# Attention and highway layer on one core: queries in 1 KB rows, transposes by row half, score and state matmuls mixed anew, a new order of work

## The chip, the cores and the metric

The kernel runs on one core of a Trainium2 chip. The core has a matrix engine (PE; its weight loads are shown apart as PEld), a vector engine (DVE), a scalar engine (ACT), a third elementwise engine (POOL) and a queue engine (SP) that issues transfers; 16 DMA engines move the data. The metric is the device time of one execution in microseconds. Before the change it was 109.42 us (median of 3 runs, 109.22 to 109.61).

## The reference, cut to what matters

Inputs: `q`, `k`, `v` of shape (4, 8, 768, 64), a decay `lam` per head, and two 512 x 512 weight matrices with a bias. Everything is float32.

```python
for b in range(nb):                       # blocks of 64 positions
    intra = (qb @ kb.T) * Dmask           # Dmask[i, j] = lam ** (i - j) for i >= j
    intra = intra @ vb
    inter = (qb * lam ** (pos + 1)) @ kv_state
    out[:, :, block] = intra + inter
    kv_state = lam ** 64 * kv_state + (kb * lam ** (63 - pos)).T @ vb
x = out as (3072, 512)                    # 4 batches x 768 positions, 8 heads x 64
H = relu(x @ w_h);  T = sigmoid(x @ w_t + b_t)
result = T * H + (1 - T) * x              # = x + T * (H - x)
```

The block length of 64 doesn't bind: the kernel scales q by `lam**t` and v by `lam**-t` and uses blocks of 128 positions.

## The kernel before, in words

**Tiles.** One tile is 256 positions of one batch with all 8 heads; there are 12 (n = 0 to 11, three in a row belong to one batch). Head pairs (`hp`, 4 of them) share the 128 partitions, `e` is the head within a pair. Position `2p + j` lies on partition p, so the upper and lower 64 partitions are the two blocks of 128 positions (`b`).

**Steps of a tile**, by their tokens: `Lk`, `Lq`, `Lv` load a half (four heads, 256 KB) each, in rows of 512 bytes. `CK` casts k to bf16, `CQ` and `CV` scale and cast q and v; most stand on POOL. `TK`, `TQ` (line 209) turn k and q on PE with eight 128 x 128 transposes each, and `EK`, `EQ` copy them out of PSUM. `SS.n.e` (lines 222 and 227) issues 16 score matmuls of one `e` in turn with 16 state matmuls of one block; each of these uses a quarter of the array. `KE` copies the running state out (512 columns, half of them zeros, so that one full-array matmul serves a head pair). `M` (line 261) masks the scores on DVE, four per tile. `I` (line 277) is q times the state, `A` (line 287) masked scores times v, both added in PSUM; `D` copies the sum into `xT`. `F` (line 305) is the highway layer: eight matmuls of 256 columns for half the output features `u` and one weight matrix `w`; `G` is the sigmoid on ACT, `H` and `X` the rest on DVE. `R` (line 352) turns the result back by matmuls with an identity on half the rows of the array each, `E` copies it out and `ST` stores 512 KB. The last tile is handled in two halves of 128 positions (F.11 and F.12).

**Order.** A string, `PLAN`, lists all tokens; each engine issues its own in that order and waits on the others by semaphores. A number behind `=` is the PSUM bank. All loads and stores go through SP's queue. `Z` (line 371) are matmuls on zeros that do no work of the kernel. The buffers of each kind are counted in `BUFS`.

Of the kernel before, what the change touches and what calls it, by code (L numbers as in the profile page):

```python
# [22 lines left out]
WC.0.1.0@POOL D.0.1@ACT Lv.2.1 WC.0.1.1@DVE Z.4=0 SS.1.0=01 M.1.1.1 I.1=35 KE.1.1@ACT Lv.2.0 F.0.0.0=4 WC.1.1.0@DVE PT
M.1.0.1 Lk.3.1 F.0.1.0=6 M.1.0.0 WC.1.0.0@POOL WC.1.0.1@ACT Lk.3.0 WC.1.1.1@DVE A.1.1 A.1.0 BC F.0.0.1=1 H.0.1 Lq.3.1
D.1.1@ACT H.0.0 D.1.0@ACT F.0.1.1=0 Lq.3.0 CQ.2.2@POOL F.1.0.0=2 Lv.3.0 G.0.1@ACT CK.2.2@DVE F.1.0.1=6 Lv.3.1
G.0.0@ACT X.0.1@DVE TQ.2.2=5 Lq.4.0 X.0.0@DVE TK.2.2=4 EQ.2.2@ACT CV.2.2@POOL F.1.1.0=3 Lq.4.1 EK.2.2@DVE G.1.0@ACT
H.1.0 SS.2.0=01 Lk.4.1 H.1.1 CK.3.2@POOL SS.2.1=54 Lk.4.0 M.2.0.1 F.1.1.1=2 KE.2.0@ACT M.2.1.0 Lv.4.0 TK.3.2=3 M.2.1.1
CQ.3.2@POOL G.1.1@ACT I.2=15 M.2.0.0 Lv.4.1 A.2.1 X.1.0@DVE A.2.0 Lk.5.0 R.0=40 D.2.0@ACT D.2.1@DVE CV.3.2@POOL
TQ.3.2=6 E.0.0@ACT Lk.5.1 F.2.1.1=1 E.0.1@ACT EQ.3.2@DVE Lq.5.1 EK.3.2@ACT X.1.1@DVE F.2.1.0=5 CQ.4.2@POOL Lq.5.0
R.1=40 H.2.1 SS.3.1=62 Lv.5.0 F.2.0.0=3 CK.4.2@POOL KE.3.0@ACT M.3.1.1 Lv.5.1 E.1.1@ACT M.3.1.0 SS.3.0=52 E.1.0@ACT  # L30
H.2.0 Lq.6.0 TQ.4.2=0 KE.3.1@ACT CV.4.2@POOL M.3.0.1 TK.4.2=6 G.2.1@ACT Lq.6.1 F.2.0.1=4 M.3.0.0 EQ.4.2@ACT EK.4.2@DVE
Lv.6.0 I.3=32 A.3.0 CK.5.2@POOL A.3.1 Lk.6.1 SS.4.1=56 D.3.0@ACT D.3.1@DVE TK.5.2=0 KE.4.0@ACT M.4.1.1 Lk.6.0
F.3.0.0=2 G.2.0@ACT CQ.5.2@POOL EK.5.2@DVE Lv.6.1 SS.4.0=36 H.3.0 F.3.0.1=0 Lq.8.0 M.4.0.0 CV.5.2@POOL M.4.0.1
TQ.5.2=2 Lk.9.0 G.3.0@ACT F.3.1.0=3 X.2.1@DVE Lq.7.0 EQ.5.2@ACT X.2.0@DVE F.3.1.1=6 CQ.6.2@POOL M.4.1.0 Lq.7.1
KE.4.1@ACT I.4=14 H.3.1 G.3.1@ACT R.2=25 Lk.8.1 X.3.0@DVE A.4.0 E.2.1@ACT X.3.1@DVE A.4.1 Lk.7.1 SS.5.0=30 E.2.0@ACT
D.4.0@DVE CK.6.2@POOL SS.5.1=56 D.4.1@ACT Lk.7.0 TQ.6.2=2 M.5.0.0 KE.5.0@ACT CV.6.2@POOL TK.6.2=1 M.5.1.1 Lv.7.0
EQ.6.2@ACT F.4.1.0=4 M.5.0.1 Lv.7.1 EK.6.2@ACT F.4.0.0=3 H.4.1 Lk.8.0 M.5.1.0 I.5=62 SS.6.1=01 H.4.0 Lq.8.1 A.5.0
KE.6.0@ACT M.6.1.0 CQ.7.2@POOL R.3=45 Lv.9.1 A.5.1 M.6.1.1 SS.6.0=30 D.5.0@ACT Lv.8.0 F.4.0.1=1 M.6.0.0 D.5.1@ACT
M.6.0.1 Lk.9.1 TQ.7.2=6 G.4.0@ACT CK.7.2@POOL F.5.0.0=3 Lq.10.1 EQ.7.2@ACT F.4.1.1=2 H.5.0 Lk.10.1 E.3.1@ACT X.4.0@DVE
# [26 lines left out]
def kernel(  # L66
# [31 lines left out]
    def copy(eng, dst, src):  # L98
        if eng == "ACT":
            A.activation(dst, src, AF.Copy)  # L100
        else:
            ENG[eng].tensor_copy(dst, src)  # L102


    lam_bc = singles.tile([128, H], F32)
    A.dma_start(out=lam_bc, in_=lam.partition_broadcast(128))
# [4 lines left out]
    blank = singles.tile([128, 512], BF16)  # L111
    V.memset(blank, 0.0)
# [53 lines left out]
    def get(*key):  # L166
        return made[key]
# [256 lines left out]
```

## Time and profile before

| | |
|---|---|
| median of 3 runs | 109.42 us |
| profiled execution, its span | 107.8 us |
| PE busy, of the span | 100.5 us, 93% |
| DVE, ACT, POOL busy | 83.4, 70.1, 55.6 us |
| moved by DMA | 27.6 MB, 256 GB/s over the span |

The profile is one execution. The span runs from the first to the last instruction of the program; the runs' times hold 1.6 us more than it (109.42 - 107.8). The chain of waits follows the work back from the last instruction. Each of its rows has a start, a length and the work. In the groups of instructions a row ends with the busy time, the mean length of one, and the idle time before them with what ended it. A matmul's own length there (some 200 to 270 ns) is latency, since matmuls are pipelined; what one costs in a stream is read from the lengths of the pieces in the chain.

### The profile page before, as it was taken

The numbers are of one execution on the slowest core, as the hardware profiler recorded it, in microseconds if no ns is written. First come the engines' busy times: TensorE is split into PE (matmuls) and PEld (weight loads), VectorE is DVE, ScalarE is ACT, GpSimd is POOL, SyncE is SP. The second block draws the span as 40 slices with busy tenths as digits, with TensorE's granted clock in tenths as the row PEclk, the third lists the DMA queues.
The fourth block names the chain that finished last, engine by engine and source line by source line (L and its number), as shares of the span: only waits on it lengthen the run. The fifth ranks groups of instructions, "written<-read, shape, count | busy, mean of one in ns | idle before, by whom it ended". The sixth has DMA issues, their size and how long they took to land.

```text
span 107.8 us, 4970 instructions
## 1 busy us (share of the span) xinstructions
PE 100.5 (93%) x2190; PEld 81.0 (75%) x2190; DVE 83.4 (77%) x140; ACT 70.1 (65%) x129; POOL 55.6 (52%) x46
## 2 busy tenths in 40 slices
PE   4998999999999999999999999999999899999950
PEld 1333655488987888889889889889898688899940
DVE  1053495879699987999995997999977978958860
ACT  2213347485875588499669758957697778587940
POOL 6028342127889887985468593999770600000000
PEclk9999999999999999999999999999999999999996
DMA  1799999999999999999999999999979334108264
GB/s 29 191 304 289 292 356 389 324 292 266 288 288 263 312 295 291 276 291 281 292 298 285 272 360 309 306 289 342 355 220 317 141 138 158 43 6 316 79 239 150
DMA packets 42701, 27.59 MB, mean 256 GB/s; under 512 B 1588, under 2 KB 38712, under 8 KB 42680
## 3 DMA queue, kind: packets, MB, share of 16 engines
q1 hardware_dynamic: 42528, 27.27, 86.7%
q8 instruction: 17, 0.28, 1.1%
q14 instruction: 4, 0.03, 0.1%
q10 hardware_dynamic: 152, 0.01, 0.1%
HBM read 20.98 MB, written 6.29 MB: 253 GB/s over the span
## 4 chain that ended last, share of the span: by engine, by line
PE 74%; DVE 10%; DMA 5%; issue 3%; POOL 1%; SPq 1%; ACT 1%; POOLq 0%; DVEq 0%
PE bt L305 18%; PE bh L305 17%; PE bs L222 7%; PE bx L352 6%; PE bo L287 6%; DMA qf<-in_q_dram 5%; DVE m L261 5%; PE bqtr L209 5%; PE bspin L371 5%; PE bktr L209 4%; PE bo L277 3%; DVE hm L310 2%; DVE th L323 2%; PE kv L227 2%; POOL qb L195 1%
## 5 line engine op out<-in xcount | busy, mean ns | idle before, releaser
L305 PEld LDWEIGHTS <-w_b 128*128 128x128 bf16 x416 | 36.4, 98 | 5.3 <-issue 0.9
L261 DVE TENSOR_TENSOR m<-bs,tri 128x512 bf16<-128x512 f32 x48 | 31.1, 683 | 2.8 <-PE bs L222 2.6
L195 POOL TENSOR_TENSOR qb<-qf,pow_q 128x1024 bf16<-128x1024 f32 (+1 forms) x13 | 23.5, 1810 | 9.4 <-DMA qf<-in_q_dram 8.7
L319 ACT ACTIVATE bt<-bt,bt_col 128x256 f32<-128x256 f32 (+1 forms) x52 | 22.0, 432 | 7.9 <-PE bt L305 4.4
L305 PE MATMUL bt<-xT,w_b 128*128 128x256 bf16 (+1 forms) x208 | 24.5, 265 | 0.7 <-issue 0.5
L305 PE MATMUL bh<-xT,w_b 128*128 128x256 bf16 (+1 forms) x208 | 25.0, 265 | 0.0
L195 POOL TENSOR_TENSOR vs<-vf,pow_v 128x1024 bf16<-128x1024 f32 x10 | 19.0, 1903 | 8.8 <-DMA vf<-in_v_dram 6.4
L310 DVE SCALAR_TENSOR_TENSOR hm<-bh,xT 128x512 bf16<-128x512 f32 (+1 forms) x26 | 16.5, 644 | 3.3 <-PE bh L305 2.4
L323 DVE TENSOR_TENSOR th<-bt,hm 128x512 bf16<-128x512 f32 (+1 forms) x26 | 16.5, 644 | 2.1 <-ACT bt L319 2.0
L371 PE MATMUL bspin<-blank,id 128*128 128x512 bf16 x45 | 13.4, 447 | 1.4 <-POOL id masks.py:199 1.4
L222 PE MATMUL bs<-qT,kT 64*64 64x128 bf16 x384 | 13.9, 218 | 0.4 <-PE bspin L371 0.2
L100 ACT ACTIVATE ss<-kv 128x512 bf16<-128x512 f32 x15 | 9.0, 597 | 7.5 <-PE bs L222 6.3
L102 POOL CAST kb<-kf 128x1024 bf16<-128x1024 f32 (+1 forms) x10 | 9.9, 994 | 6.0 <-DMA kf<-in_k_dram 6.0
L222 PEld LDWEIGHTS <-kT 64*64 64x64 bf16 x384 | 10.9, 106 | 2.6 <-issue 1.1
L100 ACT ACTIVATE xT<-bo 128x512 bf16<-128x512 f32 x16 | 9.2, 597 | 4.4 <-PE bo L287 4.4
L100 ACT ACTIVATE o<-bx 128x512 f32<-128x512 f32 x19 | 10.5, 596 | 1.3 <-PE bx L352 1.3
L100 ACT ACTIVATE qT<-bqtr 128x1024 bf16<-128x1024 bf16 (+1 forms) x10 | 9.8, 980 | 1.8 <-PE bqtr L209 1.8
L371 PEld LDWEIGHTS <-id 128*128 128x128 bf16 x45 | 4.5, 110 | 7.1 <-issue 2.8
L287 PE MATMUL bo<-m,vs 64*64 64x128 bf16 x384 | 9.1, 219 | 0.4 <-DVE m L261 0.4
L227 PE MATMUL kv<-vs,kb 64*64 64x64 bf16 x320 | 9.3, 196 | 0.0
L100 ACT ACTIVATE kT<-bktr 128x1024 bf16<-128x1024 bf16 (+1 forms) x7 | 6.8, 970 | 2.1 <-PE bktr L209 2.1
L287 PEld LDWEIGHTS <-vs 64*64 64x64 bf16 x384 | 6.5, 106 | 2.1 <-issue 1.2
(50 smaller groups left out, 111.1 us busy)
## 6 DMA issues: line engine op xcount, KB each, us to landing
kf<-in_k_dram SPq DMA_DIRECT2D x24, 256.0 KB, 5.3
vf<-in_v_dram SPq DMA_DIRECT2D x24, 256.0 KB, 5.3
qf<-in_q_dram SPq DMA_DIRECT2D x24, 256.0 KB, 5.7
out_dram<-o SPq DMA_DIRECT2D x11, 512.0 KB, 4.8
w_f<-in_moe_w_h_dram SPq DMA_DIRECT2D x2, 512.0 KB, 6.0
w_f<-in_moe_w_t_dram SPq DMA_DIRECT2D x2, 512.0 KB, 8.4
out_dram<-oh SPq DMA_DIRECT2D x2, 128.0 KB, 2.0
out_dram<-oq SPq DMA_DIRECT2D x1, 256.0 KB
```

Source lines behind the costliest of these rows:

```text
L100: A.activation(dst, src, AF.Copy)
L102: ENG[eng].tensor_copy(dst, src)
L195: ENG[eng].tensor_tensor(dst, in0=get(src, n)[:, heads(p)].rearrange("p h (j d) -> p h j d", j=J), in1=pw[:, n % NST, heads(p), :, None].t ...
L222: T.matmul(get("s", n, e, hp // 2)[half(b), hp % 2, j, :], lhsT=get("kT", n)[half(e), hp, j, half(b)], rhs=get("qT", n)[half(e), hp, b * C ...
L227: T.matmul(kv[half(e), hp, half(e)], lhsT=get("kb", n)[half(b), j, 2 * hp + e, :], rhs=get("vs", n)[half(b), 2 * hp + e, j, :], start=firs ...
L261: V.tensor_tensor(new(("m", n, e, u), [128, 2, J, C]), in0=get("s", n, e, u), in1=tri[:, None].to_broadcast([128, 2, J, C]), op=ALU.mult)
L287: T.matmul(get("o", n, b)[half(e), hp, :], lhsT=get("vs", n)[half(b), 2 * hp + e, j, :], rhs=get("m", n, e, u)[half(b), hp % 2, j, :], sta ...
L305: T.matmul(t[:, r, :], lhsT=w_b[w][:, kc, (2 * u + r) * 128:(2 * u + r + 1) * 128], rhs=get("xT", *g)[:, kc, :], start=(kc == 0), stop=(kc ...
L310: V.scalar_tensor_tensor(new(("hm", g, u), [128, 2, z * C], tag=f"hm{z}"), in0=get("h", g, u), scalar=0.0, in1=get("xT", *g)[:, 2 * u:2 * ...
L319: A.activation(dst[:, r, :], src[:, r, :], AF.Sigmoid, bias=bt_col[:, 2 * u + r:2 * u + r + 1])
L323: ENG[eng].tensor_tensor(new(("th", g), [128, NP, z * C], tag=f"th{z}")[:, 2 * u:2 * u + 2, :], in0=get("tt", g, u), in1=get("hm", g, u), ...
L371: T.matmul(t, lhsT=id128, rhs=blank, start=True, stop=True)
```

## The change

- **q in rows of 1 KB.** A partition now holds four positions in a row of four heads: the partition number's lowest bit tells which four heads. A load of half of q fills every second partition. The powers of `lam` for q have a table of their own (`tq_i`, `odd`, `q_ln`), for which `lam` is loaded twice more. Columns of q come out in another order; `tri` and `take` (`D`) are adapted, and score and `I` matmuls read every second column of the turned q.
- **Transposes by row half.** k and q are each turned by 16 transposes on 64 rows of the array, alternately on the lower and the upper half; each half has a PSUM bank, which holds k and q. One copy per half (`EB`) takes both out.
- **New mixes.** `SP.n.0` holds the 16 scores of e = 1, eight of e = 0 and the 16 state matmuls of the first block; `SP.n.1` the other eight scores and the second block's state.
- **Compact state.** Only the two used quarters of a head pair's state are kept (256 columns); `I` is eight quarter-array matmuls per block instead of four of the full array.
- **Lasting banks.** The seven PSUM banks are allocated once; the state and a side strip for `Z` and the bias share the eighth.
- **Loads.** Six load buffers instead of five, a third `qb`, weights loaded by column halves (rows of 1 KB), and after the first three tiles instead of after the first two.
- **A new order**, with 92 `Z` matmuls of 248 columns instead of 45 of 512.

Cut to its core:

```diff
-Lk.0.0 Lv.0.1 Lv.0.0 Lq.0.0 Lk.0.1 Lq.0.1 Lv.1.1 CK.0.0@POOL Lq.1.0 Z.12=0 TK.0.0=0 Lq.1.1 CV.0.0@DVE Lk.1.0
+Lv.0.1 Lq.0.1 Lq.0.0 Lv.0.0 CQ.0.1@POOL CV.0.0@POOL CV.0.1@POOL Z.26 B Lk.0.0 Lk.0.1 Lk.1.1 Lq.1.1 CK.0.0@POOL
...
-BUFS = dict(kf=5, qf=5, vf=5, kb=3, qb=2, vs=3, kT=2, qT=2, m=8, ...
+BUFS = dict(kf=6, qf=6, vf=6, kb=3, qb=3, vs=3, kqT=2, m=8, ...
...
+        if x == "q":
+            nc.sync.dma_start(out=new((x + "f", n), [128, 4, 4 * D], F32)[p::2], in_=src.rearrange("h (g i) d -> g h (i d)", i=4))
...
-                T.transpose(t[:, i, j, :], get(x + "b", n)[:, j, h:h + 2, :], id128)
...
+                for r in range(2):
+                    i = hp * J + j
+                    T.transpose(t[r][:, 0, 64 * i:64 * i + 64], kb[half(r), j, 2 * hp:2 * hp + 2, :], id128[half(r), half(r)])
...
+    def evac_t(n, r, eng):
+        copy(eng, new(("kqT", n), [128, 2, 2, 512])[:, r], get("kq", n, r))
...
+    def queries(n, e, hp, b):
+        x, z = divmod(hp, 2)
+        return get("kqT", n)[half(e), b, 1, 256 * z + x:256 * z + 256:2]
...
-        T.matmul(kv[half(e), hp, half(e)], lhsT=get("kb", n)[half(b), j, 2 * hp + e, :],
+        T.matmul(kv[half(e), hp], lhsT=get("kb", n)[half(b), j, 2 * hp + e, :],
...
+    def piece(n, x, bk):
...
+        if x == 0:
+            near = [(hp, j) for hp in range(2) for j in range(J)]
+            for hp in range(NP):
+                for j in range(J):
+                    for b in range(2):
+                        score(n, 1, hp, j, b)
+                    if j == 0:
+                        for _ in range(4):
+                            state(n, 0, *st.pop(0))
+                    else:
+                        for b in range(2):
+                            score(n, 0, *near[0], b)
+                        near.pop(0)
+        else:
+            for hp in (2, 3):
+                for j in range(J):
+                    for b in range(2):
+                        score(n, 0, hp, j, b)
+                    if n % NST < NST - 1:
+                        for _ in range(4):
+                            state(n, 1, *st.pop(0))
...
+            for hp in range(NP):
+                for e in range(2):
+                    T.matmul(get("o", n, b)[half(e), hp, :], lhsT=get("ss", n, b)[half(e), hp, :], rhs=queries(n, e, hp, b),
+                             start=o_first(n, b, e), stop=True, skip_group_check=True)
```

**SP's queue at the start.** Before (kf, vf, qf are the load buffers of k, v and q, w_f those of the weights):

```order
L178 DMA vf_109<-in_v_dram 128x4x128
L178 DMA kf_136<-in_k_dram 128x4x128
L182 DMA w_f_94<-in_moe_w_h_dram 128x2x512 x2
L182 DMA w_f_95<-in_moe_w_t_dram 128x2x512 x2
L178 DMA kf_277<-in_k_dram 128x4x128
```

After:

```order
L210 DMA kf_252<-in_k_dram 128x4x128
L210 DMA vf_358<-in_v_dram 128x4x128 x2
L213 DMA w_f_106<-in_moe_w_h_dram 128x4x256
L213 DMA w_f_107<-in_moe_w_t_dram 128x4x256
L213 DMA w_f_106<-in_moe_w_h_dram 128x4x256
L208 DMA qf_414<-in_q_dram 64x4x256 x2
```

The first weight was the 13th transfer on this queue, behind tiles 0 and 1; now it is the 19th, behind the whole of tiles 0, 1 and 2, and the fourth weight stands behind tile 3.

**PE, the transposes of k and the mix of scores and state in tile 4.** Before (kb is k, vs the scaled v, kT and qT the turned k and q, bs the scores, kv the state):

```order
L209 LDWEIGHTS kb_312
L209 MATMUL bktr<-id_67,kb_312 128x128
L209 LDWEIGHTS kb_312
L209 MATMUL bktr<-id_67,kb_312 128x128
```

```order
L222 LDWEIGHTS kT_140
L222 MATMUL bs<-qT_165,kT_140 64x128
L227 LDWEIGHTS kb_312
L227 MATMUL kv<-vs_310,kb_312 64x64
L222 LDWEIGHTS kT_140
L222 MATMUL bs<-qT_165,kT_140 64x128
L227 LDWEIGHTS kb_312
L227 MATMUL kv<-vs_310,kb_312 64x64
```

After (pb with its number is a PSUM bank, kqT the turned k and q):

```order
L249 LDWEIGHTS kb_308
L249 MATMUL pb_114<-id_69,kb_308 128x64
L249 LDWEIGHTS kb_308
L249 MATMUL pb_116<-id_69,kb_308 128x64
```

```order
L271 LDWEIGHTS kqT_246
L271 MATMUL pb_114<-kqT_246 64x128
L271 LDWEIGHTS kqT_246
L271 MATMUL pb_114<-kqT_246 64x128
L271 LDWEIGHTS kqT_246
L271 MATMUL pb_112<-kqT_246 64x128
L271 LDWEIGHTS kqT_246
L271 MATMUL pb_112<-kqT_246 64x128
```

Transposes have half as many columns and alternate between two banks. Where each score was followed by one state matmul, a group of two scores of e = 1 is now followed by four state matmuls or, as in the last rows, by two scores of e = 0 (another bank).

More of the change, by code (lines that the diff above doesn't have):

```diff
@@ L23 @@
[L23 to L27, printed above, removed]
@@ L102, in copy @@
             ENG[eng].tensor_copy(dst, src)
-    lam_bc = singles.tile([128, H], F32)
-    A.dma_start(out=lam_bc, in_=lam.partition_broadcast(128))
+    lam_all = singles.tile([128, H + 4], F32)
+    A.dma_start(out=lam_all[:, 0:H], in_=lam.partition_broadcast(128))
+    for x in range(2):
+        A.dma_start(out=lam_all[x::2, H:H + 4], in_=lam[4 * x:4 * x + 4].partition_broadcast(64))
     bt_r = singles.tile([KC, 128], F32)
@@ L159, in new @@
         return made[key]
+    banks = [ps.tile([128, 512], F32, name=f"pb{i}") for i in range(7)]
     def bank(key, i, shape, dtype=F32):
         if key not in made:
-            made[key] = ps.tile(shape, dtype, tag=f"b{i}", name=f"b{key[0]}", bufs=1)
+            free = shape[1:]
+            size = 1
+            for x in free:
+                size *= x
+            v = banks[i] if dtype == F32 else banks[i].bitcast(dtype)
+            v = v[0:shape[0], 0:size]
+            if len(free) > 1:
+                names = "abcd"[:len(free)]
+                v = v.rearrange(f"p ({' '.join(names)}) -> p {' '.join(names)}", **dict(zip(names, free)))
+            made[key] = v
         return made[key]
@@ new lines, in trans_q, with keys @@
+    def trans_q(n, bk):
+        t, qb = turned(n, bk), get("qb", n)
+        for z in range(2):
+            for i in range(4):
+                for r in range(2):
+                    y = z * 4 + i
+                    T.transpose(t[r][:, 1, 64 * y:64 * y + 64], qb[half(r), i, 2 * z:2 * z + 2, :], id128[half(r), half(r)])
+    def evac_t(n, r, eng):
+        copy(eng, new(("kqT", n), [128, 2, 2, 512])[:, r], get("kq", n, r))
+    def keys(n, e, hp, j, b):
+        i = hp * J + j
+        return get("kqT", n)[half(e), b, 0, 64 * i:64 * i + 64]
@@ L257, in evac_s @@
     def evac_s(n, b, eng):
-        copy(eng, new(("ss", n + b, 1 - b), [128, NP, 128]), kv)
+        copy(eng, new(("ss", n + b, 1 - b), [128, NP, 64]), kv)
     def mask(n, e, u):
@@ L361, in store_r, with bias, spin, spin4 @@
         nc.sync.dma_start(out=out[i:i + 2 * C].rearrange("(b p) f -> p b f", p=C), in_=get("o_sb", n).rearrange("p b j f -> p b (j f)"))
-    def bias(bk):
-        t = bank(("bt",), bk[0], [128, KC])
-        T.transpose(t, bt_r, id_f)
-    def spin(r, bk, idle=[0]):
-        idle[0] += 1
-        t = bank(("spin", idle[0]), bk[0], [128, 512])
-        for _ in range(r):
-            T.matmul(t, lhsT=id128, rhs=blank, start=True, stop=True)
+    def bias():
+        made["bt",] = pair[:, 256:256 + KC]
+        T.transpose(get("bt"), bt_r, id_f)
+    def spin(r, n=[0]):
+        for _ in range(r):
+            T.matmul(side, lhsT=id128, rhs=blank[:, 0:248], start=n[0] == 0, stop=True, skip_group_check=True)
+            n[0] += 1
+    def spin4(r, bk):
+        for i in range(r):
+            for x in range(2):
+                for y in range(2):
+                    T.matmul(banks[bk[x]][half(y), 0:64], lhsT=id128[half(x), 0:64], rhs=blank[half(x), 0:64], start=True, stop=True)
     DO = {
```

204 lines of the change are left out of this document (106 added, 98 removed).

## The prediction, as put on record

> **What bounds the kernel now.** I read the page's slices and busy times first, then the busy times by stage, then the chain of waits.
>
> ```profile
> span 107.8 us, 4970 instructions
> PE 100.5 (93%) x2190; PEld 81.0 (75%) x2190; DVE 83.4 (77%) x140; ACT 70.1 (65%) x129; POOL 55.6 (52%) x46
> PEclk9999999999999999999999999999999999999996
> DMA  1799999999999999999999999999979334108264
> PE 74%; DVE 10%; DMA 5%; issue 3%; POOL 1%; SPq 1%; ACT 1%; POOLq 0%; DVEq 0%
> ```
>
> Two resources look full: PE at full clock, and the DMA engines for the first three quarters. Which one sets the end is told by the stages (PE, PEld, DVE, ACT, POOL busy, clock, DMA share, GB/s), cut where the chain meets its first `F`:
>
> ```profile
> 0.00:22.41 22.41, 19.96 (x252) 10.35 (x253) 11.44 (x22) 8.46 (x14) 8.77 (x17) 1.00 0.97 272
> 22.41:65.00 42.59, 42.41 (x1008) 36.88 (x1006) 37.92 (x61) 31.29 (x56) 31.65 (x21) 1.00 1.06 291
> 65.00:84.00 19.00, 18.76 (x494) 16.75 (x487) 16.93 (x27) 14.85 (x26) 13.25 (x8) 1.00 1.00 305
> 84.00:104.33 20.33, 19.38 (x451) 17.05 (x448) 16.66 (x31) 15.47 (x34) 1.90 (x1) 1.00 0.35 128
> 104.33:107.81 3.48, 0.00 (x0) 0.00 (x0) 0.42 (x1) 0.00 (x0) 0.00 (x0) 0.74 0.55 196
> 0.00:22.41 22.41, 13.44 (x45) 4.53 (x45) 1.00 0.97 272
> ```
>
> The last row is `Z` (line 371) alone: 13.4 of the first 22.4 us are filler, so **the head is bound by the loads**. From 22.41 to 104.33 no filler runs and PE is busy but for a little over 1 us, also in the 20 us after the loads have ended, so **the middle is bound by PE's stream**: what it no longer has to stream comes off the end. DVE is next, 71.5 of these 81.9 us (87%). The tail of 3.5 us is the last copy and store.
>
> The chain gives what a piece costs in the stream (start, length, work):
>
> ```profile
> 22.41 1.75 PE bh L305 x16
> 38.11 0.98 PE bh L305 x8
> 39.09 0.15 PE bs L222 x2
> 39.30 0.04 PE kv L227 x3
> 39.44 0.04 PE bs L222
> 39.49 0.17 PE bs L222 x6
> 39.66 0.55 PE bqtr L209 x8
> 40.21 0.45 PE bktr L209 x8
> 40.66 0.87 PE bt L305 x8
> 47.95 0.45 PE bo L277 x8
> 48.40 0.57 PE bx L352 x32
> 48.97 0.57 PE bo L287 x32
> 94.77 1.04 PE bx L352 x64
> ```
>
> An `F` takes 0.87 (1.75 for two), eight 128-column transposes or `I` matmuls 0.45. 32 matmuls of `R`, 64 columns on alternate row halves, take 0.57, but 64 take 1.04: 32 more cost 0.47, and the first 0.10 is the switch from one use of the array to another. The switch is seen again in 0.98 and 0.55 for pieces that cost 0.87 and 0.45 without one. A whole `SS` runs from 39.09 to 39.66, 0.57, and `A` takes 0.57; both begin with a switch into quarter-array use, whose first row shows 0.15. I take 0.13 for any switch, so 0.44 for `SS` and 0.43 for a tile's `A`.
>
> **The change part by part: PE.** Pieces from the first `F` on, counted in both orders, with these prices:
>
> - `F`: 44 of 0.87 and 8 of half the columns in both, 42.0 and 42.0.
> - Transposes: before 20 pieces of 0.45 (tiles 2 to 11), 8.9. After, 16 matmuls of 64 columns on alternate row halves, the form of line 352: half of 0.47, 0.235. Tiles 3 to 11 (tile 2's stand ahead of the first `F`): 18 x 0.235 = 4.2. **-4.7**.
> - Scores and state: an `SS` lasts as long as 16 scores of 128 columns on one row half, the two column halves together (8 x 128 columns, 0.44); its states, on the other row half, fill half of that. In `SP.n.0` both halves carry 1024 column steps, 0.44; in `SP.n.1` 512, 0.22. Before 20 x 0.445 = 8.9, after 9 x 0.445 + 10 x 0.22 = 6.2. **-2.7**.
> - `I`: eight quarter-array matmuls in pairs are four steps of 128 columns, 0.215, as before. 3.8 becomes 3.4, and `A` 4.7 becomes 4.3, both because pieces went ahead of the first `F`. **-0.8**.
> - `R` 6.1 in both.
> - Switches: 47 before, 63 after, 6.1 becomes 8.2. **+2.1**.
>
> Sum 80.5 before and 74.4 after, **-6.1**. Before's 80.5 stand against 81.9 measured, so waits were 1.4 us. The bounds of the unseen prices: the transposes cost from 0.235 to 0.45 (no pairing), the mixes from 0.22 to 0.44 for `SP.n.1`, a strided read of q from nothing to twice the length. I take the low end each time, being nearest to rows of the same shape (line 352; lines 222 and 227).
>
> [...]
>
> **The head.** First uses of load 1, load 5, load 12 and the first two weights, and `lam`'s load on ACT's queue:
>
> ```profile
> 0.80 0.45 ACTq L106 DMA_DIRECT2D lam_bc<-in_lam_dram  x1
> ...
> 5.65 0.61 POOL L102 CAST kb<-kf 128x512 bf16<-128x512 f32 x1 [3.00 <-DMA kf<-in_k_dram]
> ...
> 9.15 0.63 ACT L100 ACTIVATE kb<-kf 128x512 bf16<-128x512 f32 x1 [3.09 <-DMA kf<-in_k_dram]
> ...
> 15.46 1.06 ACT L100 ACTIVATE kb<-kf 128x1024 bf16<-128x1024 f32 x1 [0.64 <-DMA kf<-in_k_dram]
> ...
> 18.12 1.17 POOL L102 CAST w_b<-w_f 128x512 bf16<-128x512 f32 x2 [3.35 <-DMA w_f<-in_moe_w_h_dram]
> ```
>
> And three groups (times of one in ns behind the comma):
>
> ```profile
> L195 POOL TENSOR_TENSOR vs<-vf,pow_v 128x1024 bf16<-128x1024 f32 x10 | 19.0, 1903 | 8.8 <-DMA vf<-in_v_dram 6.4
> L261 DVE TENSOR_TENSOR m<-bs,tri 128x512 bf16<-128x512 f32 x48 | 31.1, 683 | 2.8 <-PE bs L222 2.6
> L100 ACT ACTIVATE ss<-kv 128x512 bf16<-128x512 f32 x15 | 9.0, 597 | 7.5 <-PE bs L222 6.3
> ```
>
> A load of 256 KB in 512-byte rows takes (15.46 - 5.65) / 11 = 0.89; two weights of 512 KB in 2 KB rows take 2.66, so 0.67 per 256 KB. A q load in 1 KB rows lies between; I take 0.77. Load 18 lands at 5.65 + 11 x 0.89 + 6 x 0.77 = 20.1. It is v of tile 2, which POOL scales in 1.9. At 22.0 the state of tile 2 can run (0.13 + 0.44), and the first weight, landed at 21.6, is cast by 22.2. The first `F` is at **22.5**, where it was; but more attention stands behind it, which is how 6.1 could leave the middle. The fourth weight stands behind tile 3: landed at 20.1 + 3 x 1.54 + 4 x 0.89 + 2 x 0.77 + 1.54 = 31.4. Until its `F.0.0.1` PE has 9.6 us of work (32.1), and a cast takes 0.6: no stall worth counting. Tile 4's v lands near 36.5, and is scaled at 38.4; PE reaches its `SP` at about 38.5. From there a tile is 2 x (0.89 + 0.89 + 0.77) = 5.1 us of loads against 6.5 us of PE, so loads run ahead.
>
> **Costed at nothing.** New one-time sums on DVE and two small `lam` transfers (two more issues of 0.45 on ACT's queue) delay the first q scaling by some 0.9 us; they hide behind the wait for the loads of tiles 1 and 2 (without that cover, +0.9). `KE` with half its columns falls from 597 ns to between 300 and 597, to ACT's gain alone, which is busy 75% of the middle. DVE loses 4 `KE`, 3 `D` and a k cast and gains 5 result copies, about -2; the new banks and the sixth load buffer wait for nothing that is late. DVE stays at 87% of a shorter middle, so its 683 ns masks make as many collisions: waits of 2.2 instead of 1.4. The tail ends in the same copy and store, 3.5.
>
> **Sum.** 22.5 + 74.4 + 2.2 + 3.5 = 102.6 against the profiled 107.8. Around the span lie 109.42 - 107.8 = 1.6, so **104.2 us**, 4.8% less than the median.
>
> **The rivals.**
>
> - *DVE and ACT take PE's place.* For it: DVE's 87%, and an order packed more closely. Against: its work shrinks along with PE's. If waits reach 5 us: 107.0.
> - *The transposes don't pair*, so that this part doesn't do what it says: 18 x 0.21 = 3.8 more, 108.0. Against it stands line 352, the same shape on alternate halves and banks.
> - *Slower: the q load by every second partition runs at half the rate.* For it: no transfer of the trace fills 64 partitions. Mechanism: 256 KB then takes twice 0.89, 1.0 more than I take. Six such loads put the first `F` at 28.5; then a tile's loads take 7.1 us against PE's 6.5, and over eight tiles some 2 us more is lost: 104.2 + 6 + 2 = **112.2**. It decides from a q load of about 1.6 us on, where six cost 5.
> - *Slower: strided reads of q at half rate*: nine tiles x 0.66 and 16 x 0.215, 9.4 more, 113.6.
>
> [...]
>
> **How the numbers follow.** The forecast, with waits up to 3.7, holds 0.58 (102.5 to 105.7 as its own range); DVE's and ACT's waits 0.16 (to 108); unpaired transposes 0.08; the two slower ones and their like (a buffer that comes free late, say) 0.15; 0.03 is left for gains beyond 102.5. A measurement tells 0.3% from no change. Within that falls little but the edges between the cases, 0.05; faster 0.80, slower 0.15. The range goes from 102.0 (waits gone) to 109.5, where one in ten is left above.
>
> **What would show it.** In the new profile: 16 transposes in about 0.25 us; `SP.n.0` near 0.45 and `SP.n.1` near 0.22; the first `F` at 22.5; PE's last matmul near 99 with waits of 2 us; q loads at 0.8 us. A first `F` after 24, or PE idle in the middle for over 4 us with DVE or a load as its releaser, would make it wrong.

## The result, and the profile after

The changed kernel takes **122.53 us** (median of 4 runs, 120.75 to 123.83) where the kernel before took 109.52 on the same chip. The ratio is **1.106, interval 1.094 to 1.118**: 11% slower, where 104.2 us was forecast. The profiled execution took 120.75, its span is 119.0. (Some runs of these kernels were disturbed; the ratios and the differences between kernels given below leave those out, the medians don't, and the traces of experiments 1, 2, 10 and 11 are of such runs.)

The page of the changed kernel, head, clock and chain:

```profile
span 119.0 us, 5721 instructions
PE 100.6 (85%) x2541; PEld 81.5 (69%) x2541; DVE 83.6 (70%) x139; ACT 81.9 (69%) x135; POOL 54.8 (46%) x47
PEclk9999999958999999999999999999999999999999
q8 instruction: 20, 0.33, 1.1%
PE 54%; ACT 17%; issue 12%; DVE 5%; DMA 5%; POOL 3%; SPq 1%; POOLq 0%; DVEq 0%; ACTq 0%
```

PE is busy as long as before (100.6 us) but for 85% of a longer span. The chain runs over ACT for 17% of it, where it was 1%, and over `issue` for 12%, where it was 3%: PE or ACT standing still without a semaphore that the profile shows. Of these 14 us, 7.0 are PE's. The row q8, 20 packets that carry instructions, is dealt with below. By stage (PE, PEld, DVE, ACT, POOL busy, clock, DMA share, GB/s), cut at the first `F` (29.91) and at PE's last matmul (115.39):

```profile
0.00:29.91 29.91, 23.23 (x485) 17.19 (x485) 11.68 (x24) 11.51 (x17) 17.51 (x25) 0.94 0.97 275
29.91:65.00 35.09, 31.81 (x853) 26.20 (x848) 29.97 (x47) 29.71 (x48) 25.00 (x16) 1.00 1.05 294
65.00:84.00 19.00, 16.39 (x480) 13.12 (x478) 15.60 (x25) 15.27 (x24) 10.41 (x8) 1.00 0.87 280
84.00:115.39 31.39, 29.21 (x734) 25.03 (x731) 26.39 (x45) 25.01 (x48) 1.85 (x1) 1.00 0.28 106
115.39:119.00 3.61, 0.00 (x0) 0.00 (x0) 0.00 (x0) 0.38 (x1) 0.00 (x0) 1.00 0.38 128
```

Against the forecast's span of 102.6 that makes 16.4 us in four terms. The first `F` comes at 29.91 instead of 22.5: +7.4. From there PE is busy 31.81 + 16.39 + 29.21 = 77.4 instead of 74.4: +3.0. It stands still for 85.5 - 77.4 = 8.1 instead of 2.2: +5.9. The tail is 3.6 instead of 3.5: +0.1.

What PE waited for longest (us in total, times, longest):

```profile
PE kv L276 <- issue: 3.5, 3, 1.7
PE pb L271 <- issue: 1.7, 3, 1.0
PE pb L257 <- issue: 1.5, 1, 1.5
PE kv L432 <- POOL id masks.py:199: 1.4, 1, 1.4
PE pb L395 <- DVE th L386: 1.0, 1, 1.0
PE pb L368 <- ACT xT L103: 0.9, 2, 0.4
PE pb L368 <- DVE xT L105: 0.8, 2, 0.5
PE pb L339 <- ACT xT L103: 0.8, 2, 0.5
PE kv L428 <- DMA bt_r<-in_moe_b_t_dram: 0.6, 1, 0.6
PE pb L257 <- ACT xT L103: 0.6, 1, 0.6
```

The waits on `id` and `bt_r` lie in the first 8 us, ahead of the first tile's work. Of the others two groups stand out, `issue` and `xT`, and they are two causes.

**Cause A: `D` became dear.** `take` copies the output of a tile's attention from PSUM to `xT`. In the changed kernel it also puts the 128 positions back in order, by writing every fourth column. Its groups in the changed kernel, on ACT and on DVE:

```profile
L103 ACT ACTIVATE xT<-pb 128x512 bf16<-128x512 f32 x19 | 24.7, 1329 | 7.4 <-PE pb L349 7.2
L105 DVE CAST xT<-pb 128x512 bf16<-128x512 f32 x5 | 6.5, 1301 | 0.4 <-PE pb L349 0.4
```

and in the kernel before:

```profile
L100 ACT ACTIVATE xT<-bo 128x512 bf16<-128x512 f32 x16 | 9.2, 597 | 4.4 <-PE bo L287 4.4
L102 DVE CAST xT<-bo 128x512 bf16<-128x512 f32 x8 | 5.5, 685 | 0.6 <-PE bo L287 0.6
```

The same shape takes 1329 ns for 597, and 1301 for 685. PE's waits on `xT` add up to 3.3 us (with a fifth row of 0.2).

**Cause B: PE stops in the middle of pieces.** The stalls called `issue` lie between two matmuls of the same piece of work (one token of the order) with no wait between them in the program. These windows of the changed kernel end each at the start of such a stall; what matters is how many matmuls (the x behind PE) had been run by then:

```profile
0.00:15.83 15.83, 13.36 (x223) 9.80 (x223) 5.07 (x14) 4.32 (x8) 8.73 (x18) 1.00 0.85 235
0.00:21.78 21.78, 17.73 (x351) 13.27 (x351) 8.19 (x19) 6.65 (x12) 12.64 (x21) 1.00 0.93 259
0.00:28.81 28.81, 23.02 (x479) 17.05 (x479) 11.68 (x24) 10.56 (x17) 16.41 (x24) 0.94 0.97 273
0.00:47.67 47.67, 39.97 (x862) 30.69 (x863) 27.18 (x48) 25.96 (x41) 31.02 (x34) 0.96 1.00 282
0.00:65.97 65.97, 56.00 (x1374) 44.01 (x1375) 42.62 (x73) 41.88 (x66) 43.48 (x41) 0.97 1.00 281
0.00:76.35 76.35, 64.90 (x1630) 51.32 (x1631) 51.11 (x85) 50.98 (x79) 47.65 (x43) 0.98 0.99 283
```

223, 351, 479, 862, 1374, 1630: every stall of PE over 0.5 us that is called `issue` comes after 95 + 128 k matmuls (to within one). A matmul is two rows of PE's instruction list, a weight load and the matmul itself, so the stalls stand **256 rows apart**. The row q8 says what is 256 rows long: 20 packets with 0.33 MB are 16 KB each, and the page's 2541 weight loads and 2541 matmuls, 5082 rows (the recorded texts count one more), make 19.9 pieces of 256 (16 KB over 256 rows, so 64 bytes a row). Before there were 17 packets for 4380 rows, 17.1 pieces:

```profile
q8 instruction: 17, 0.28, 1.1%
```

So PE's list comes in pieces of 256 rows over the same DMA engines as the loads (the page counts q8 and the loads' q1 on the same 16), and in this trace PE stood at a piece's edge where it got there before the piece. For each stall longer than 0.5 us, worked out from the trace's packets and matmuls:

```
PE stops   fetch packet   took   PE goes on   packet's start to PE   stall
15.82      14.76          1.14   17.32        2.56                   1.50
21.77      20.80          1.07   23.51        2.71                   1.75
28.80      26.99          1.19   29.71        2.72                   0.91
47.67      45.77          1.21   48.48        2.71                   0.80
65.96      64.24          1.12   66.95        2.72                   1.00
76.34      74.56          1.02   76.88        2.32                   0.54
```

Three shorter ones add 0.5, so the stalls are 4.2 us ahead of the first `F` and 2.8 behind it, 7.0 in all. The trace before has one edge stall, at 85.57, after 1758 matmuls (95 + 128 x 13 to within one):

```profile
PE bt L305 <- issue: 0.5, 1, 0.5
```

In the changed kernel a piece of the list was used 2.3 to 2.7 us after its packet had started, and while loads run the packets start 1 to 3.5 us after PE has entered the piece before. From edge to edge that is 4.4 to 6.2 us where PE stalled: **PE had run the 256 rows in 3.4 to 5.3 us of these, and waited for the rest**. 32 transposes of the new form and their weight loads are 64 rows in 0.57 us, an `F` is 16 rows in 0.87.

The prices of the PE pieces themselves came out as forecast. The two transposes of a tile, and the stretches from `I` through `SP.n.1` to the next `F` in tiles 7 and 8, in the chain of the changed kernel:

```profile
57.83 0.41 PE pb L257 x16
58.24 0.26 PE pb L249 x16
...
69.08 0.46 PE pb L339 x12
69.66 0.09 PE pb L271 x3
69.91 1.85 PE pb L368 x16
...
78.92 0.46 PE pb L339 x12
79.49 0.23 PE pb L271 x6
79.72 0.98 PE pb L368 x8
```

`SP.8.1`, the row of 0.23, has no state matmuls (tile 8 is the last of its batch). With 16 of them, in tile 7, the stretch takes 69.91 - 69.08 = 0.83 us instead of 79.72 - 78.92 = 0.80: they cost next to nothing beside the scores.

One warning on this view: the chain also has `issue` at 55.08 (1.03 us) and three times more for about 1 us, ahead of an ACT instruction. There ACT was running another copy, at 55.08, 82.21 and 98.96 one of `xT` with its 1.3 us; that is ACT's own work, not a stall of PE.

### The profile page after: what moved, and what is told of

The parts are those of the page before. It is cut to its first block, busy times and chain, and to the rows that moved or that the text cites. A ratio compares the mean times of both kernels' runs of the same rounds, so it can differ in the third digit from the quotient of the medians.

```text
span 119.0 us, 5721 instructions
## 1 busy us (share of the span) xinstructions
PE 100.6 (85%) x2541; PEld 81.5 (69%) x2541; DVE 83.6 (70%) x139; ACT 81.9 (69%) x135; POOL 54.8 (46%) x47
## 2 busy tenths in 40 slices
DMA packets 37890, 27.65 MB, mean 232 GB/s; under 512 B 1764, under 2 KB 35048, under 8 KB 37864
## 4 chain that ended last, share of the span: by engine, by line
PE 54%; ACT 17%; issue 12%; DVE 5%; DMA 5%; POOL 3%; SPq 1%; POOLq 0%; DVEq 0%; ACTq 0%
PE pb L368 23%; ACT xT L103 8%; PE pb L271 6%; PE pb L349 5%; DMA qf<-in_q_dram 5%; PE kv L432 5%; PE pb L339 4%; ACT pb L382 4%; PE pb L415 3%; PE pb L257 3%; PE pb L249 3%; DVE th L386 3%; PE kv L276 2%; DVE xT L105 2%; ACT ss L103 2%
## 5 line engine op out<-in xcount | busy, mean ns | idle before, releaser
L368 PE MATMUL pb<-xT,w_b 128*128 128x256 bf16 (+1 forms) x416 | 47.3, 265 | 2.2 <-ACT xT L103 0.9
L324 DVE TENSOR_TENSOR m<-pb,tri 128x512 bf16<-128x512 f32 x48 | 31.2, 685 | 11.5 <-PE pb L271 8.9
L228 POOL TENSOR_TENSOR qb<-qf,pow_q 128x1024 bf16<-128x1024 f32 (+1 forms) x12 | 21.6, 1802 | 20.4 <-DMA qf<-in_q_dram 20.4
L103 ACT ACTIVATE xT<-pb 128x512 bf16<-128x512 f32 x19 | 24.7, 1329 | 7.4 <-PE pb L349 7.2
L235 POOL TENSOR_TENSOR vs<-vf,pow_v 128x1024 bf16<-128x1024 f32 (+1 forms) x14 | 23.1, 1656 | 8.6 <-DMA vf<-in_v_dram 4.0
L382 ACT ACTIVATE pb<-pb,bt_col 128x256 f32<-128x256 f32 (+1 forms) x52 | 22.5, 441 | 2.7 <-PE pb L368 1.8
L386 DVE TENSOR_TENSOR th<-pb,hm 128x512 bf16<-128x512 f32 (+1 forms) x26 | 16.7, 646 | 4.6 <-ACT pb L382 3.8
L103 ACT ACTIVATE kqT<-pb 128x1024 bf16<-128x1024 bf16 x13 | 13.2, 1025 | 8.1 <-PE pb L257 4.2
L373 DVE SCALAR_TENSOR_TENSOR hm<-pb,xT 128x512 bf16<-128x512 f32 (+1 forms) x26 | 16.5, 645 | 1.3 <-PE pb L368 0.4
L271 PE MATMUL pb<-kqT 64*64 64x128 bf16 x384 | 15.6, 220 | 2.1 <-issue 1.7
L432 PE MATMUL kv<-blank,id 128*128 128x248 bf16 x92 | 15.1, 328 | 1.5 <-POOL id masks.py:199 1.4
```

The source lines that it names most:

```text
L228: ENG[eng].tensor_tensor(new(("qb", n), [128, 4, 4, D])[:, :, ys], in0=get("qf", n)[:, ys].rearrange("p y (i d) -> p i y d", i=4), in1=pow ...
L235: ENG[eng].tensor_tensor(new(("vs", n), [128, H, J, D])[:, hs], in0=get("vf", n)[:, hs].rearrange("p h (j d) -> p h j d", j=J), in1=pow_v[ ...
L271: T.matmul(get("s", n, e, hp // 2)[half(b), hp % 2, j, :], lhsT=keys(n, e, hp, j, b), rhs=queries(n, e, hp, b), start=True, stop=True)
L324: V.tensor_tensor(new(("m", n, e, u), [128, 2, J, C]), in0=get("s", n, e, u), in1=tri[:, None].to_broadcast([128, 2, J, C]), op=ALU.mult)
L368: T.matmul(t[:, r, :], lhsT=w_b[w][:, kc, (2 * u + r) * 128:(2 * u + r + 1) * 128], rhs=get("xT", *g)[:, kc, :], start=(kc == 0), stop=(kc ...
L373: V.scalar_tensor_tensor(new(("hm", g, u), [128, 2, z * C], tag=f"hm{z}"), in0=get("h", g, u), scalar=0.0, in1=get("xT", *g)[:, 2 * u:2 * ...
```

## The experiments

The theory is A and B together. The rivals are A alone, B alone, and waits that the profile doesn't show (semaphores, loads) in place of B.

### 1. D without the stepped write

```diff
- xT[...].rearrange("p n (g i) -> p n i g", i=4)  <-  o.rearrange("p n (i g) -> p n i g", i=4)
+ xT[...].rearrange("p n (g i) -> p n g i", i=4)  <-  o.rearrange("p n (i g) -> p n g i", i=4)
```

> The changed kernel, but `take` (D) reads the accumulator with a step of 32 columns and writes xT without a step, where it read without a step and wrote with a step of 4 columns (8 bytes). Theory A (the stepped write is what makes D dear): xT copies on ACT fall from 1329 ns to 600-650 and on DVE from about 1120 to 600; ACT's busy time from 81.9 us to about 68; PE's waits on xT (0.9 + 0.8 + 0.8 + 0.6 + 0.2 = 3.3 us) nearly go, and the time falls by 3 to 8 us, to 113-118 us. Theory B (PE starves at every 256th row of its instruction list): the stalls in the middle of pieces stay, at the rows 190 + 256 k, with 6 to 8 us in sum. Rival (any reordering copy costs this, whichever side has the step): xT stays above 1100 ns and the time stays within 1 us.

Measured: 121.6 us (119.65 to 123.5), ratio to before 1.098 (1.087 to 1.109). The copy on ACT, and then the longest two of PE's waits in this run:

```profile
L103 ACT ACTIVATE xT<-pb 128x512 bf16<-128x512 f32 x19 | 11.1, 597 | 10.4 <-PE pb L349 10.3
```

```profile
PE kv L276 <- issue: 5.1, 4, 1.8
PE pb L271 <- issue: 4.8, 3, 2.0
```

The copy is cheap again, also with a step of 128 bytes in what it reads, and yet the time hardly moves: 1 us by the ratios, and the intervals of this run and of the changed kernel overlap. The forecast of 113 to 118 was a miss. The stalls at edges are 13.2 us in the traced run, of 122.64 us, where they were 7.0; they stand at the same edges (after 862, 1374, 1502, 1630 and 1758 matmuls, and now after 1246 too) and are longer:

```profile
0.00:61.76 61.76, 52.44 (x1246) 41.20 (x1247) 37.91 (x68) 33.72 (x61) 40.45 (x39) 0.97 1.04 291
```

PE came to the next edge sooner and waited there for what it had waited for at `xT` before. That accounts for 3.3 of the 6.2 us by which the stalls grew; the rest is not explained. So B is not a second small loss but what sets the pace once A is gone.

### 2. D as a plain copy, the order put right by the stores

```diff
- copy(eng, xT[...].rearrange("p n (g i) -> p n i g", i=4), o.rearrange("p n (i g) -> p n i g", i=4))
+ copy(eng, xT[...], o)
- out[i:i + 2 * C].rearrange("(b p) f -> p b f", p=C)                     # one store of 512 KB
+ out[i + b * C:i + b * C + C].rearrange("(g i) f -> i g f", i=4)         # for b in 0, 1
```

> The changed kernel, but `take` (D) is a plain copy, and the order of the rows is put right by the stores: each 256-row store becomes two, whose output rows are addressed as (i g) instead of one after the other. D costs what it did in the kernel before (597 ns on ACT). Theory A: the same time as with the contiguous write, within 1 us, 113-118 us; if the read with a step is dear too, this one is faster by up to 24 x 0.5 us on the path, of which some 3 us would show. Theory B: the stalls at rows 190 + 256 k stay, 6 to 8 us in sum, so that the kernel stays slower than before by 3 us or more, although its PE pieces are shorter by 6 us. Rival (D alone explains the loss): 104-106 us, as predicted.

Measured: 149.1 us, ratio 1.352 (1.336 to 1.367). Neither theory had that. The copies took 596 ns as expected; the stores are what broke. The end of this run, when only stores were left:

```profile
125.00:140.00 15.00, 0.44 (x6) 0.21 (x3) 0.83 (x3) 0.75 (x3) 0.00 (x0) 0.65 0.26 101
```

DMA share 0.26, 101 GB/s: that is as much as four of the sixteen engines fully at work (0.26 x 16 = 4.2), and the store's outer dimension is now 4. That the one follows from the other is the author's reading; it was not shown by itself. At that rate a store of 262,000 bytes takes 2.6 us, and loads stand behind it in SP's queue (the issue of the load at 81.20, behind four stores, took 2.50 us; those of the loads at 54.66 to 56.73 took 0.54 to 0.63). For A and B the run says only that PE stalls at the same edges, for 10.4 us in all, and in the head about as long as in the first experiment (5.2 us against 4.3).

### 3. The kernel before with the stepped write

```diff
- copy(eng, xT[...], o)
+ copy(eng, xT[...].rearrange("p n (g i) -> p n i g", i=4), o.rearrange("p n (i g) -> p n i g", i=4))
```

> The kernel before, with one edit: `take` (D) writes xT with a step of 4 columns, as the changed kernel does; it leaves out the reordering that would make up for it, so the output rows stand in another order. Theory A: xT copies on ACT go from about 600 ns to about 1330, on DVE from about 600 to 1120; D stands between A and F on the path, but other pieces are ordered in between: 24 copies x 0.7 us = 17 us more work on two engines, of which I expect 3 to 7 us in the time, 112.5-116.5 us. If the price came from the PSUM bank or from the fewer tiles instead of from the step: no change, 109.5 us.

Measured: 114.87 us (114.73 to 114.92), ratio 1.050 (1.043 to 1.057), +5.4 us.

The groups of `D` in this run, and PE's longest wait:

```profile
L100 ACT ACTIVATE xT<-bo 128x512 bf16<-128x512 f32 x16 | 20.6, 1339 | 4.4 <-PE bo L287 4.4
L102 DVE CAST xT<-bo 128x512 bf16<-128x512 f32 x8 | 10.4, 1302 | 0.6 <-PE bo L287 0.6
```

```profile
PE bh L306 <- ACT xT L100: 2.0, 4, 0.7
```

1339 and 1302 ns in another kernel, with other banks and tiles: the step is the cause of the price, and it alone costs the kernel before 5.4 us. A holds, as a theory of what `D` costs.

### 4. The kernel before with 96 rows more

```diff
- T.matmul(t, lhsT=id128, rhs=blank, start=True, stop=True)
+ for c in ((0, 104), (104, 208), (208, 312), (312, 412), (412, 512)) if idle[0] == 1 else ((0, 512),):
+     T.matmul(t[:, slice(*c)], lhsT=id128, rhs=blank[:, slice(*c)], start=True, stop=True)
```

> The kernel before, with the first 12 filler matmuls of 512 columns each cut into five that cover the same columns: 48 more matmuls, 96 more rows in PE's instruction list, the same columns streamed, all of it before the first loads have landed. Every later instruction moves by 96 rows against the pieces of 256 in which PE's list is fetched. Theory B: PE now stalls in the middle of pieces at rows 190 + 256 k of the new list, where the 256 rows before it took less than 4.6 us to run; the rows and times of the trace before give 4 to 5 us of such stalls instead of 0.5, so 112.5-114.5 us. Rival (the stalls come from semaphores or from the loads, not from the list's pieces): no change beyond 0.5 us, 109-110 us.

Measured: 113.05 us (112.06 to 115.65), ratio 1.030 (1.021 to 1.039), +3.3 us by the ratio. The first `F` is not later (22.05 against 22.24), and the two long stalls come after 1118 and 1630 matmuls (windows of this run that end at them):

```profile
0.00:55.45 55.45, 51.87 (x1118) 41.13 (x1119) 41.41 (x70) 32.83 (x57) 33.42 (x32) 1.00 1.03 282
0.00:78.67 78.67, 73.18 (x1630) 59.95 (x1630) 60.74 (x100) 48.49 (x84) 51.13 (x44) 1.00 1.03 286
```

Both are 95 + 128 k again (k = 8 and 12) while the program around them has moved on by 48 matmuls. They last 1.66 and 1.86 us, 3.5 in all, where the kernel before had 0.5, and head the list of PE's waits:

```profile
PE bs L222 <- issue: 3.5, 2, 1.9
```

48 filler matmuls that stream nothing more cost 3.3 us, far from where they stand. No theory of semaphores or loads gives that; B does, and gave stalls of 4 to 5 us.

### 5. Whole transposes: fewer rows, a longer stream

```diff
- for r in range(2):
-     T.transpose(t[r][:, 0, 64 * i:64 * i + 64], kb[half(r), j, 2 * hp:2 * hp + 2, :], id128[half(r), half(r)])
+ T.transpose(t[0][:, 128 * i:128 * i + 128], kb[:, j, 2 * hp:2 * hp + 2, :], id128)
  (the same for q into t[1]; `keys` and `queries` read the new places; D writes without a step)
```

> The changed kernel with the contiguous write of D, and with k and q transposed whole: 16 transposes of 128 rows and 128 columns for a tile instead of 32 of 64 rows and 64 columns (keys in one bank, queries in the other). PE's instruction list loses 384 of its 5083 rows, one and a half of the 256-row pieces; PE's stream gets longer, by 24 x (0.45 - 0.235) = 5 us less some switches of the array, 3.5 to 5 us. Theory B (the pieces of the list arrive every 4 to 6 us while loads run, and that is the bound): the time falls all the same, by 3 to 6 us, to 115-118 us, and the stalls at rows 190 + 256 k fall from 13.2 us to 6-9. Rival (PE's stream is the bound, as the prediction took it): 3.5 to 5 us slower than with the contiguous write, 125-127 us.

Measured: **113.91 us** (113.19 to 115.35), ratio 1.038 (1.026 to 1.049), 6.4 us under the first experiment (113.7 against 120.1) although PE has more to stream. Its stages up to the first `F` and from there to PE's last matmul:

```profile
0.00:24.95 24.95, 22.02 (x438) 17.39 (x438) 10.89 (x24) 9.82 (x17) 14.54 (x22) 1.00 0.95 271
24.95:108.79 83.84, 79.03 (x1916) 67.16 (x1912) 70.13 (x115) 59.83 (x118) 40.53 (x26) 1.00 0.81 244
```

PE streams 79.0 us here and stands still for 4.8; stalls at edges are 4.5 us in the whole run instead of 13.2, and the first `F` comes 4.7 us earlier than in the first experiment. The part of the change that the forecast made its largest gain, -4.7 us, turned out its largest loss in this order of work.

### 6. Without the loads of tiles 6 to 11

```diff
+ if n >= 6:
+     new((x + "f", n), None)      # the tile's buffer, with what an earlier tile left in it
+     return
```

> The changed kernel with the contiguous write of D, and without the loads of k, q and v from tile 6 on: those tiles compute on what tiles 0 to 5 left in the six load buffers, so the output is not the reference's from there. The loads are then over at about 45 us. Theory B1 (the fetch of a piece of PE's list stands behind load packets on the DMA engines): the fetches after that start within 0.3-1.3 us of the row 190 + 256 k that calls for them, instead of 1.3-3.6, a piece is there 2.9-3.7 us after it was called for instead of 4-6.2, the stalls from there on fall from 8-9 us to under 2, and the time falls by 6 to 9 us, to 112.5-115.5. Rival B2 (a fetch takes 4-6 us in any case): the same stalls and 121-122 us.

Measured: 113.43 us (112.56 to 114.59), ratio 1.033 (1.023 to 1.043), 7 us under the first experiment. From 45 us on its stage reads

```profile
45.00:107.56 62.56, 60.39 (x1730) 51.22 (x1722) 55.78 (x94) 47.86 (x98) 26.17 (x16) 1.00 0.26 97
```

The stalls at edges from there on are 1.1 us instead of 8.9. The packets of PE's list now start 1.2 us on average after PE has entered the piece before (0.5 to 1.2 in eight of eleven, 2.0 to 2.6 in three that fell into a store), where it was 2.5 with loads on the DMA engines. So the fetch stands behind the load packets (B1); a fixed time for a fetch (B2) is out. What sets the length of that wait is not shown.

This run also shows the forecast's own middle: from the first `F` (30.10) to PE's last matmul (107.56) PE is busy 75.3 us and stands still for 2.2, where 74.4 and 2.2 had been worked out. That the second figure is the same is luck: the forecast meant collisions with DVE's masks, while here 1.1 us are edges and 1.0 is the last gate.

### 7. Without the late fillers

```diff
- ... W.0.1 Z.4 TK.1=15 ... Z.12 A.0.1=4 ... Z.5 SP.1.0=051 ... Z.4 TQ.2=14 ... Z.10 I.2.0=1 ...
+ ... W.0.1 TK.1=15 ... A.0.1=4 ... SP.1.0=051 ... TQ.2=14 ... I.2.0=1 ...
```

> The changed kernel with the contiguous write of D, and without the 35 filler matmuls (70 rows of PE's list) that its order keeps between the first tile and the first F. Theory C (the fillers, 5 us of PE at a partly halved clock, stand in PE's queue ahead of pieces that are already late): the first F comes 1.5 to 3 us earlier and the time falls by as much, to 118.5-120. Theory B alone: in the head the pieces of the list arrive every 6.2 us whatever PE does in between, so the first F moves only by what 70 rows fewer mean, 70/256 x 6.2 = 1.7 us, and the rest is luck with where the boundaries fall: 118-122. Without fillers the granted clock of the stage before the first F may fall below the 0.91 of the changed kernel; a clock below 0.8 there with no gain in time would say that they are needed.

Measured: 119.76 us (119.22 to 121.11), ratio 1.092 (1.083 to 1.101). The first `F` is at 27.65 instead of 29.63, and the stage ahead of it runs at a low clock:

```profile
0.00:27.65 27.65, 20.22 (x451) 16.42 (x451) 10.98 (x24) 9.96 (x17) 14.80 (x23) 0.77 0.97 274
```

2.0 us earlier at a clock of 0.77 (0.94 with the fillers, in the first experiment), so the fillers kept the clock. What they cost isn't told by this: the edge stalls ahead of the first `F` fell as well, from 4.3 to 1.5 us, and the ratio is within the first experiment's interval. Both theories allowed the result.

### 8. Both edits together

> Both edits together: whole transposes and no late fillers, 4629 rows in PE's list against 5083 in the changed kernel and 4381 before. Theory B: the pieces are fewer by almost two, and the gains add up: 112-117 us, still not under the kernel before, whose list has one piece less. Rival (PE's stream): 121-125 us.

Measured: 114.18 us (112.48 to 115.51), ratio 1.035 (1.021 to 1.048), the same as with whole transposes alone. First `F` at 24.59, 0.4 us earlier; stalls 4.7 us. The gains don't add up. That with fewer rows the fillers were no longer in the way is a reading of this, not shown.

### 9. Whole transposes with the stepped write

> The changed kernel with whole transposes and with its own D, which writes xT in steps of 8 bytes. Beside the run with whole transposes and contiguous write (113.9 us) it gives the price of the stepped write where PE's list stalls it little (4.5 us in sum instead of 13.2). Theory A and B together (D's price was hidden in the changed kernel, because a later D only gave the next piece of PE's list time to arrive): xT copies on ACT back at about 1330 ns, and the time 3 to 6 us above 113.9, 117-120 us, although in the changed kernel the contiguous write gained only 1 us. Rival (D's price is hidden in this order of the work, whatever PE does): 113.5-115 us.

Measured: 119.56 us (117.3 to 121.59), against 113.91 (113.19 to 115.35) with the contiguous write; the ranges don't meet. So the stepped write costs time here as well. How much is known only roughly: 3.6 us by the one run that can be compared (117.3 against 113.7), where it was 5.4 in the kernel before and some 1 us in the changed kernel. The copy on ACT and PE's longest wait on it in this run:

```profile
L103 ACT ACTIVATE xT<-pb 128x512 bf16<-128x512 f32 x19 | 24.7, 1329 | 8.4 <-PE pb L347 8.2
PE pb L366 <- ACT xT L103: 1.4, 3, 0.6
```

The edge stalls are 2.0 us instead of 4.5. A and B cover each other: what PE waits for at `xT` it doesn't wait for at the next edge.

### 10. The fewest rows

```diff
- for e in range(2): T.matmul(o[half(e), hp, :], lhsT=ss[half(e), hp, :], rhs=queries(n, e, hp, b), ...)
+ T.matmul(o[:, hp, :], lhsT=ss[:, hp, :], rhs=queries of both halves, ...)     # ss 128 x 128, zero off the diagonal
- T.matmul(side, lhsT=id128, rhs=blank[:, 0:248], ...)                            # Z.26, Z.11, Z.18, Z.2
+ T.matmul(banks[6], lhsT=id128, rhs=blank, ...)                                  # 512 columns: Z.13, Z.5, Z.9, Z.1
```

> Contiguous write, whole transposes, no late fillers, and two edits more that take rows from PE's list at about the same streaming time: the product of queries and state with whole 128 x 128 state blocks, zero beside the diagonal, 4 matmuls instead of 8 for half a tile (160 rows less, KE becomes two copies of 64 partitions), and the fillers of the head in 512 columns instead of 248 (58 rows less). 4411 rows in all, 672 fewer than in the changed kernel, 30 more than before. Theory B: the stalls fall from 4.7 us to about 3, the time to 111-113.5 us. Rival (the row count no longer matters, the stream does): 114-115 us as with whole transposes and no late fillers.

Measured: 113.99 us (112.33 to 115.05), ratio 1.031 (1.018 to 1.043): no gain that can be told. The edge stalls did fall, from 4.7 to 2.6 us, but PE was busy for 81.0 us from the first `F` on (78.6 in experiment 8), with a granted clock of 0.82 in the 9.4 us behind it, and that `F` came at 25.64. Between 4628 and 4410 rows no gain from the count can be seen; whether the clock hid one is open. A miss.

### 11 and 12. The kernel before with 16 rows more, and with balanced mixes at two tiles

> The kernel before with 8 of its first 12 filler matmuls cut in two: 16 more rows of PE's list, the same columns, in the head. The other direction of the run with 96 rows: the one stall at a piece's edge in the trace before (0.5 us at row 3517) falls into a stretch whose 256 rows take longer. Theory B: no stall is left after the first F, 0.3 to 0.6 us faster, 108.9-109.2 us. Rival: no difference, 109.5.

Measured: 109.38 us, ratio 0.998 (0.994 to 1.001). No difference can be told. Its trace has 1.2 us of stalls at three other edges, where none was expected. Half a microsecond couldn't be planned with B.

```diff
- SS.3.1=62 ... SS.3.0=52 ... SS.9.1=61 ... SS.9.0=36
+ SP.3.0=625 ... SP.3.1=2 ... SP.9.0=613 ... SP.9.1=6
```

> The same, and one part of the change alone at the two tiles where a bank is free for it: tiles 3 and 9 take their scores and states in the changed kernel's two unequal pieces (24 scores with the first half's states, then 8 scores with the second half's), the number of PE rows unchanged. The price that the prediction gave this part: 0.445 + 0.22 instead of 2 x 0.445 for a tile, so 0.45 us for two tiles, if the third bank is free in time: 108.4-108.8 us. Rival (masks set the pace there, or the early bank costs a wait): no gain over the run with 16 rows.

Measured: 110.07 us, ratio 1.002 (0.998 to 1.006). The mixes' gain, 0.45 us, doesn't show; that is at the edge of what these runs can tell. The trace has a reason for tile 3. In its chain `SP.3.0` runs from 37.41 to 38.18 and `SP.3.1` from 39.16 to 39.54, 0.77 and 0.38 us, together as long as two `SS` of 0.57. In the first of them PE stands for 0.16 us until DVE has emptied the third bank (37.53), which is the rival that was named.

No version tried is faster than the kernel before.

## Why the prediction was wrong, point by point

- **"The middle is bound by PE's stream: what it no longer has to stream comes off the end."** This is the step that failed. The middle was bound by PE's stream only as long as its list arrived in time. The forecast quoted `issue` with 3% of the chain and did not ask what it was; the trace before holds one such stall, 0.5 us. 256 rows took 4.5 us or more there while loads ran. The change was to take 6 us from the stream (it took 5.4 without loads beside it) and adds 700 rows: 20 pieces of the list instead of 17, and more of them dense. No term of the sum counted instructions, and PE stood at the edges of these pieces for 7.0 us, 13.2 in the first experiment's trace. The forecast's own sign of being wrong, PE idle for over 4 us, came (8.1), but with the list and one copy as its causes, not DVE or a load.
- **The prices of the PE pieces were right.** 16 transposes took 0.26, and 0.41 with the switch, `SP.8.1` 0.23; and without loads beside it the stream took 75.3 us against 74.4. That reading q with a step of two columns costs nothing was the forecast's estimate, and no row of before shows it; `SP.8.1`, whose eight scores read q so, took 0.23 where half an `SS` of before, without a step, had been priced at 0.22.
- **`D` was not priced at all.** The part on what was "costed at nothing" counts three fewer `D` on DVE and doesn't look at how the remaining ones write. Their write in steps of 8 bytes took 1329 ns for 597 on ACT and 1301 for 685 on DVE: 24 copies x 0.7 = 17 us on two engines, 5.4 us of the time where PE's list is no limit (the third experiment).
- **Waits of 2.2 us** were 8.1: 2.8 at edges, 3.3 on `xT`, 1.0 on the last gate, the rest small. The collisions with DVE's masks that the 2.2 stood for are not among PE's longest waits.
- **The first `F` at 22.5** was 29.91. The edges cost 4.2 us of these 7.4. The first weights landed at 22.6 instead of 21.6, so that the load term was 1 us short. With whole transposes and no late fillers the first `F` stood at 24.59, with 0.6 us of stalls ahead of it. What share the late fillers and the attention behind the weights have in the remaining 2 us is not shown.
- **PE's 77.4 us** against 74.4: 0.9 is the miss of the prices (75.3 without loads). The other 2.1 may lie in pieces of work that a stall cuts in two; that is argued, not shown.
- **The rivals.** q loads of 64 partitions took 0.72 to 0.79 us in the head, from one landing to the next, so the half-rate rival is out, and so is the strided read. The transposes pair (16 in 0.26, where eight whole ones took 0.45). DVE and ACT didn't take PE's place by their load, but ACT by one copy did, in part. The slower side had 0.15, for mechanisms none of which came; that a list can be late was not among them.
- **What each cause did** can be said only for kernels, not as two addends: 121.5 us as changed, without A 120.1, without part of B 117.3 (one run), without both 113.7. The last 4.3 us to the kernel before are, by the two traces, the later head (24.95 against 22.24, 2.7 us) and 4.8 us of idle PE against 1.35, less 1.7 us of shorter stream and 0.2 of tail.

A single edge cost up to 2.4 us (in the trace of the sixth experiment, `PE pb L260 <- issue`), and the edges of one run 13.2 us (the first experiment).

## What to carry to other kernels

Count a PE change in instructions as well as in streamed columns: while loads kept the DMA engines full, PE got 256 rows (128 matmuls with their weight loads) per 4.4 to 6.2 us wherever it stalled in the changed kernel, and a form that halves the stream by doubling the matmuls can lose: the transposes by row half cost 6.4 us here (120.1 against 113.7). Look for stalls called `issue` in the middle of pieces and compare how many matmuls lie between them; here it was a multiple of 128 at every one over 0.5 us, and the list was late. And price a copy anew when its access pattern changes, even if its shape, type and count don't: here the copy on ACT took 597 ns with the step on the side that reads PSUM and 1329 with it on the side that writes, and the order put right by stores with an outer dimension of 4 took the kernel to 149.1 us.

## What the runs showed of the hardware that was not expected

- PE's list is fetched in 16 KB packets (20 of them, 0.33 MB; 17 and 0.28 in the kernel before) by the DMA engines that carry the loads. A packet mostly takes 0.9 to 1.4 us; PE went on 2.2 to 3.0 us after its start in the stalls of all these runs, and it mostly starts 1 to 3.6 us after the piece before was entered while loads run, 0.5 to 1.2 when they don't.
- 48 matmuls more in the head of a program, at the same streamed columns, cost 3.3 us tens of microseconds later, by moving the edges; 8 more cost nothing that can be told.
- An ACT copy of 128x512 from PSUM took 597 ns with steps of 128 bytes in what it reads, and 1329 ns with steps of 8 bytes in what it writes to SBUF as bf16.
- Stores whose outer dimension is 4 ran at 101 GB/s, with a DMA share of 0.26, as much as about four of the sixteen engines (0.26 x 16 = 4.2).
